# Order of weight conversions and splits in a retention, MLP and top-1 expert kernel

## The chip, the cores and the metric

The kernel runs on one core of a Trainium2 chip. TensorE (PE) multiplies matrices, VectorE (DVE), ScalarE (ACT) and GpSimd (POOL) work on elements, and SyncE (SP) issues most transfers. Each engine runs its own instructions in program order and waits for others by semaphores. The metric is the device time of one execution in microseconds. Before the change three runs took 579.2, 579.36 and 579.41 us.

## What is computed

Three stages in float32, each feeding the next; the weights `w_in` and `w_out` of the MLP come as float64.

```python
# retention attention, 2 batches x 8 heads, 768 positions, head size 64
intra = ((q @ k.T) * Dmask) @ v              # within a block of 64 positions
inter = (q * lam_pow) @ kv_state             # state carried over blocks
# MLP on x [1536, 512], hidden size 2048
h = maximum(x @ w_in, 0.0);  x = (h * h) @ w_out
# top-1 mixture of 8 experts, hidden size 1024
logits = x @ w_gate;  e_idx = argmax(logits, axis=1)
gate_w = softmax(logits)[arange(N), e_idx]
eom = 1 / (1 + exp(-(x @ w_output_gate)))
for e in range(8):
    mask = e_idx == e
    h = maximum(x[mask] @ w1[e], 0.0)
    out[mask] = gate_w[mask, None] * eom[mask, e, None] * (h @ w2[e])
```

## The kernel before

**Splitting.** To keep float32 accuracy, every operand of a big matmul is split in a high and a low part (`xTh`/`xTl`, `wih`/`wil`, `woh`/`wol`, `gh`/`gl`, `w1h`/`w1l`, `w2h`/`w2l`, `hh`/`hl`), and a product is three matmuls: high by high, low by high, high by low. A split is one cast on ScalarE (the high part) and one subtraction on VectorE or GpSimd (the low part), each 128 x 512.

**Attention** takes 12 units of 128 tokens and leaves its result, transposed and split, in `xTh` and `xTl` (512 rows in four pieces `kk` by 1536 token columns).

**MLP.** The tokens go in three chunks of 512 columns; the hidden size goes in 16 blocks `f` of 128. A step is s = 16 * chunk + f, 48 in all. `mm1(s)` is 12 matmuls (L339), `act1(s)` makes g = relu squared and splits it (L346 to L357), and `mm2(s - 2)` is 12 matmuls into four accumulators (L449), two steps behind. `split_in(s + 2)` splits a block of `w_in` (L326, L327) after `act1(s)`, `split_out(s)` a block of `w_out` within it.

**Conversion.** In the last units of attention and the first 12 steps of chunk 0 the float64 weights arrive in staging tiles `st` (SP, L107 and L110; four buffers) and are converted on the chip, two blocks a step: a scaled copy on ScalarE (L124), a shift (L125) and two combining operations on VectorE (L128 and L130, the second reads what the first wrote). The last two are kept in a list and run inside `act1` of the next step. From chunk 1 on no conversion is left, and `wol` is made by GpSimd.

**Routing.** Each chunk's result goes to memory as rows `x1d`, and the expert, position and slot of each token are worked out (`ohb`, `pos`, `pay`, `poh`, `sacc`, `sidx`, `gidx`). Tokens of an expert are fetched by indirect transfers of GpSimd (`xg`, L830), transposed by TensorE (`pt`, L850) and split into `xh`, `xl` (L855, L856) by `xpose`. For expert 0 the last tokens are picked by matmuls instead (`xt`, L717).

**Experts.** Each expert has eight blocks of 128 hidden units. `emm1(e, f)` (L884) makes `ph` in one of two PSUM buffers, then `hh` (ACT, L899) and `hl` (DVE, L900); `emm2(e, f - 2)` (L907) accumulates the output two blocks behind. The columns of `emm1` are 256 for expert 0, and 384, 256 or 192 by the token count for the others. `put` scales a result (L911) and scatters it to `out` (L912). `split1` and `split2` split the blocks of w1 and w2, each into one of 4 and 10 slots. Expert 0 also carries the rest of the routing of the last chunk in a table `late`, one list of jobs a block.

**Order.** All of it is written out by hand: an engine does its instructions in the order of the program. So an `hl` that waits for nothing still stands behind everything that VectorE was given before it.

Of the kernel before, what the change touches and what calls it, by code (L numbers as in the profile page):

```python
# [23 lines left out]
def attn_moe_kernel(ctx, tc, q, k, v, lam, w_in, w_out, w_gate, w_ogate, w1, w2, out):  # L24
# [367 lines left out]
    for u in range(NU):  # L394
# [361 lines left out]
    w1r, w2r = {}, {}
    NS = NCK * NF
    LAG = 2
    for s in range(NS + LAG):
# [19 lines left out]
        if s >= LAG:  # L779
# [82 lines left out]
    NS2 = E * NF2

    def split1(s, eng=nc.vector):
        if s < NS2:
            esplit(w1_of(*divmod(s, NF2)), *w1s[s % R1], eng)

    def split2(s, eng=nc.vector):
        if s < NS2:
# [4 lines left out]
    def emm1(e, f):
# [5 lines left out]
        def go(N):  # L880
            n = 0
            for kk in range(KC):
                for w_, x_ in ((w1h, xh), (w1h, xl), (w1l, xh)):
                    nc.tensor.matmul(out=ps[:, 0:N], lhsT=w_[:, kk, :], rhs=x_[:, kk, 0:N], start=n == 0,  # L884
                                     stop=n == 3 * KC - 1)
                    n += 1
# [41 lines left out]
    route_poh(ch, 0)  # L928
    route_poh(ch, 1)
    late = {0: [lambda: route_sum(ch), route_csb, lambda: route_poh(ch, 2)],  # L930
            1: [lambda: slot_mm(ch, [0, 1], 0, 2), lambda: slot_fin(ch, [0, 1], 0, 2), lambda: gathers(1, range(NSL))],
            2: [lambda: slot_mm(ch, [2], 0, 2), route_count, lambda: slot_fin(ch, [2], 0, 2), lambda: gathers(1, [NSL])],
            3: [lambda: route_gate(ch)],
            4: [lambda: route_gate1(ch)],
            5: [lambda: route_gate2(ch)],
            6: [lambda: slot_mm(ch, [0, 1], 2), lambda: slot_mm(ch, [2], 2), lambda: slot_fin(ch, [0, 1], 2),
                lambda: slot_fin(ch, [2], 2), lambda: route_gates(slice(0, NG))],
            7: [lambda: route_table(ch)]}
# [3 lines left out]
    def loads(s):  # L942

        while loaded[0] < NP and (loaded[0] // 2 < 4 or s + 3 >= (loaded[0] // 2 - 4) * 4 + 3):
            load_w1(loaded[0])
            loaded[0] += 1
        while loaded[1] < NP and (loaded[1] // 2 < 4 or s + 2 >= (loaded[1] // 2 - 4) * 4 + 3):
            load_w2(loaded[1])
            loaded[1] += 1
# [99 lines left out]
```

## Time and profile before

| what | value |
|---|---|
| median of three runs | 579.36 us |
| profiled execution | 580.5 us |
| its span, first to last instruction | 578.7 us |
| mean granted TensorE clock | 0.983 |
| TensorE busy | 552.3 us, 95% |
| VectorE busy | 374.0 us, 65% |
| ScalarE busy | 306.7 us, 53% |
| GpSimd busy | 153.9 us, 27% |

Busy time is the time in which an engine executes instructions; the waits of TensorE name the instruction that released it. A bracket at the end of a timeline row gives the idle time ahead of the instruction and its releaser. The granted clock is a share of full speed: 1 is 2.4 GHz, a half is 1.2 GHz.

### The profile page before, as it was taken

To read this page: it belongs to the slowest core of one execution; us is meant where nothing else is said; L and a number is where in the kernel's file an instruction comes from. 1 tells how busy PE (TensorE), PEld (TensorE's weight loads), DVE (VectorE), ACT (ScalarE), POOL (GpSimd) and SP (SyncE) were. 2 spreads that over 40 slices of the span, in tenths; PEclk is the share of its full clock that TensorE was granted. 3 is DMA by queue.
4 is the path that set the end of the run, shared out by engine and by line. 5 is a ranking of instruction groups with operands and counts; after the bars stand their busy time and mean duration, and the time that the engine had idled before them with its cause. 6 is when DMAs were issued, how large, how long until landed. Compare 5 with 4: busy or idle time off the path is not lost. (4 is left out here: it accounts for less than half of the span.)

```text
span 578.7 us, 9460 instructions
## 1 busy us (share of the span) xinstructions
PE 552.3 (95%) x3412; PEld 466.0 (81%) x3412; DVE 374.0 (65%) x744; ACT 306.7 (53%) x584; POOL 153.9 (27%) x153
## 2 busy tenths in 40 slices
PE   7999899999999999999999999899999999899994
PEld 6898777888777877887877887789898889888883
DVE  7579988998444665454565447965547649887430
ACT  4666476775544344434344335535456758886530
POOL 5788100000012132332113341223313132341101
PEclk8999998999999999999999999989999999999998
DMA  9999456568100001000000003975829477860000
GB/s 186 240 237 256 115 148 182 182 205 305 68 0 2 19 19 37 0 1 0 20 18 20 19 0 112 370 280 139 272 101 292 163 223 228 277 224 20 9 22 23
DMA packets 75043, 72.86 MB, mean 126 GB/s; under 512 B 30181, under 2 KB 61029, under 8 KB 74976
## 3 DMA queue, kind: packets, MB, share of 16 engines
q1 hardware_dynamic: 70624, 62.96, 36.9%
q0 software_dynamic: 4064, 8.91, 4.6%
q8 instruction: 42, 0.69, 0.5%
q14 instruction: 25, 0.20, 0.1%
q10 hardware_dynamic: 288, 0.10, 0.1%
HBM read 65.84 MB, written 9.29 MB: 130 GB/s over the span
## 5 line engine op out<-in xcount | busy, mean ns | idle before, releaser
L327 POOL TENSOR_TENSOR wol<-woF,woh 128x512 fp32r<-128x512 f32 x32 | 41.6, 1301 | 231.9 <-ACT woh L326 231.9
L357 DVE TENSOR_TENSOR gl<-g,gh 128x512 fp32r<-128x512 f32 x48 | 53.6, 1116 | 70.4 <-ACT gh L356 70.4
L884 PE MATMUL ph<-xh,w1h 128*128 128x192 f32 (+2 forms) x256 | 76.4, 299 | 6.0 <-PEq L1013 2.5
L339 PE MATMUL ps<-xTh,wil 128*128 128x512 f32 x192 | 76.7, 399 | 1.9 <-DVE wil L327 1.9
L339 PE MATMUL ps<-xTh,wih 128*128 128x512 f32 x192 | 77.9, 406 | 0.0
L339 PE MATMUL ps<-xTl,wih 128*128 128x512 f32 x192 | 76.5, 398 | 0.0
L449 PE MATMUL acc<-gh,woh 128*128 128x512 f32 x192 | 76.1, 396 | 0.3 <-DVE x1T L461 0.2
L449 PE MATMUL acc<-gl,woh 128*128 128x512 f32 x192 | 75.8, 395 | 0.0
L449 PE MATMUL acc<-gh,wol 128*128 128x512 f32 x192 | 75.8, 395 | 0.0
L884 PE MATMUL ph<-xl,w1h 128*128 128x192 f32 (+2 forms) x256 | 74.9, 293 | 0.1
L884 PE MATMUL ph<-xh,w1l 128*128 128x192 f32 (+2 forms) x256 | 74.9, 293 | 0.0
L900 DVE SCALAR_TENSOR_TENSOR hl<-ph,hh 128x384 fp32r<-128x384 f32 (+1 forms) x64 | 34.5, 539 | 61.8 <-ACT hh L899 60.8
L326 ACT CAST woh<-woF 128x512 fp32r<-128x512 f32 x48 | 29.7, 619 | 64.6 <-PE acc L449 62.3
L884 PEld LDWEIGHTS ph<-xh,w1h 128*128 128x128 f32 x256 | 48.9, 191 | 9.9 <-issue 6.1
L899 ACT ACTIVATE hh<-ph 128x384 fp32r<-128x384 f32 (+1 forms) x64 | 30.7, 479 | 45.0 <-PE ph L884 43.0
L346 ACT ACTIVATE r<-ps 128x512 f32<-128x512 f32 x48 | 28.5, 593 | 44.1 <-PE ps L339 44.1
L907 PE MATMUL ea<-w2h,hh 128*128 128x512 f32 x128 | 51.4, 402 | 0.0
L907 PE MATMUL ea<-w2l,hh 128*128 128x512 f32 x128 | 50.4, 394 | 0.0
L907 PE MATMUL ea<-w2h,hl 128*128 128x512 f32 x128 | 50.3, 393 | 0.0
L884 PEld LDWEIGHTS ph<-xl,w1h 128*128 128x128 f32 x256 | 48.8, 191 | 1.5 <-DVE xl L856 0.3
L860 DVE TENSOR_TENSOR w2l<-w2r,w2h 128x512 fp32r<-128x512 f32 x71 | 49.1, 691 | 0.2
L912 POOL DMA_INDIRECT out_dram<-y,sidx x23 | 24.3, 1058 | 93.3 <-ACT y L911 51.3
(177 smaller groups left out, 1135.3 us busy)
## 6 DMA issues: line engine op xcount, KB each, us to landing
w1r<-in_moe_w_dram SPq DMA_DIRECT2D x32, 512.0 KB, 5.8
w2r<-in_moe_w_dram SPq DMA_DIRECT2D x32, 512.0 KB, 6.7
st<-in_moe_w_in_dram SPq DMA_DIRECT2D x16, 512.0 KB, 3.8
st<-in_moe_w_out_dram SPq DMA_DIRECT2D x16, 512.0 KB, 4.8
q<-in_q_dram SPq DMA_DIRECT2D x24, 128.0 KB, 4.1
k<-in_k_dram SPq DMA_DIRECT2D x12, 256.0 KB, 4.6
v<-in_v_dram SPq DMA_DIRECT2D x12, 256.0 KB, 5.4
x1d<-xr SPq DMA_DIRECT2D x12, 256.0 KB, 2.0
```

What stands on the lines that cost most here:

```text
L326: nc.scalar.copy(out=hi, in_=src)
L327: eng.tensor_tensor(out=lo, in0=src, in1=hi.bitcast(F32), op=ALU.subtract)
L339: nc.tensor.matmul(out=ps, lhsT=w_[:, kk, :], rhs=x_[:, kk, tk], start=n == 0, stop=n == 3 * KC - 1)
L346: nc.scalar.activation(out=r, in_=ps, func=AF.Relu)
L357: nc.vector.tensor_tensor(out=gl, in0=g, in1=gh.bitcast(F32), op=ALU.subtract)
L449: nc.tensor.matmul(out=acc[ch][cb], lhsT=w_[:, cs], rhs=x_, start=f == 0 and i == 0, stop=f == NF - 1 and i == 2)
L860: eng.tensor_tensor(out=lo, in0=src, in1=hi.bitcast(F32), op=ALU.subtract)
L884: nc.tensor.matmul(out=ps[:, 0:N], lhsT=w_[:, kk, :], rhs=x_[:, kk, 0:N], start=n == 0, stop=n == 3 * KC - 1)
L899: nc.scalar.activation(out=hh[:, f, ts_], in_=ps[:, ts_], func=AF.Relu)
L900: nc.vector.scalar_tensor_tensor(out=hl[:, f, ts_], in0=ps[:, ts_], scalar=0.0, in1=hh[:, f, ts_].bitcast(F32), op0=ALU.max, op1=ALU.subtract)
L907: nc.tensor.matmul(out=ea[j], lhsT=h_[:, f, js], rhs=w_, start=f == 0 and i == 0, stop=f == NF2 - 1 and i == 2)
L912: nc.gpsimd.indirect_dma_start(out=out[:, :], out_offset=bass.IndirectOffsetOnAxis(ap=sidx[:, j, e:e + 1], axis=0), in_=ys[j], in_offset=N ...
```

## The change

1. `conv_w` returns the two combining operations apart, and `flush` runs the first ones of both conversions and then the second ones.
2. In steps 2 to 15, `split_in(s + 2)` runs inside `act1(s)`, after `split_out(s)` and ahead of `flush`.
3. `xTh` and `xTl` outlive the MLP. The slots of `split1` and eight of the ten of `split2` are parts of them: token columns whose chunk is done. The first four blocks of w1 and of w2 of expert 0 are split in steps 33 to 40, in the third chunk of the MLP (`ch` = 2); the subtraction is then `xTl<-w1r,xTh`.
4. In the expert loop `splits_to` splits w1 four blocks ahead and up to two blocks of w2 after each `emm1`, as far as ten blocks of w2 from the expert's start; loads follow what is split.
5. Expert 0: the matmuls of `emm1(0, 0)` that read `xl` come after those of the same pair of `kk` that read `xh`; all `poh` and the counts stand ahead of the block loop; one `slot_mm`, `slot_fin` and gather job for all three groups, in block 1; the gate in blocks 2 and 3; `xpose(1, 0)` and `xpose(1, 1)` in blocks 6 and 7 and `xpose(1, 2)` after the last `emm2`.
6. The scatters to `out` and `tab` go through disjoint views of them, so that they do not wait for each other.

```diff
+    outs = dram_disjoint_views(out, NG)
+    tabs = dram_disjoint_views(tab, 4)
+    xp = ctx.enter_context(tc.tile_pool(name="xp", bufs=1))
+    xTh = xp.tile([P, KC, NT], F32R, name="xTh")
+    xTl = xp.tile([P, KC, NT], F32R, name="xTl")
...
-        def rest():
+        def shifted():
             nc.vector.scalar_tensor_tensor(out=sh(lo), in0=dst.bitcast(U32), scalar=3, in1=sh(lo),
                                            op0=ALU.logical_shift_left, op1=ALU.bitwise_or)
+
+        def signed():
             nc.vector.scalar_tensor_tensor(out=dst.bitcast(U32), in0=sh(hi), scalar=0x80000000, in1=sh(lo),
                                            op0=ALU.bitwise_and, op1=ALU.bitwise_or)
-        return rest
+        return shifted, signed
...
+    def flush():
+        for step in range(2):
+            for r_ in rest_:
+                r_[step]()
+        rest_.clear()
...
-            nc.gpsimd.indirect_dma_start(out=tab[:, :], out_offset=bass.IndirectOffsetOnAxis(ap=sl[:, t, :], axis=0),
+            nc.gpsimd.indirect_dma_start(out=tabs[t][:, :], out_offset=bass.IndirectOffsetOnAxis(ap=sl[:, t, :], axis=0),
...
+    R1, R2 = 4, 10
+    room = [[x_[:, kk, c * NTC:(c + 1) * NTC] for x_ in (xTh, xTl)] for c in range(NCK) for kk in range(KC)]
+    w1s = [[t_.rearrange("p (k f) -> p k f", k=KC) for t_ in room[i]] for i in range(R1)]
+    w2s = room[R1:]
...
-                act1(s, lambda: (split_out(s), flush()))
+                early = 2 <= s < NF
+                act1(s, lambda: (split_out(s), split_in(s + 2) if early else None, flush()))
         if s == 0:
             split_in(3)
-        elif 2 <= s < NS - 2:
+        elif NF <= s < NS - 2:
             split_in(s + 2)
...
+        if s - 2 * NF in range(1, 9):
+            i, j = divmod(s - 2 * NF - 1, 2)
+            (split1, split2)[j](i)
...
+            mms = [(kk, w_, x_) for kk in range(KC) for w_, x_ in ((w1h, xh), (w1h, xl), (w1l, xh))]
+            if s == 0:
+                mms.sort(key=lambda m: (m[0] // 2, m[2] is xl))
...
-    split1(0)
-    split1(1)
-    split2(0)
     xpose(0, 0)
-    split1(2)
     xpose(0, 1)
...
-    route_poh(ch, 0)
-    route_poh(ch, 1)
-    late = {0: [lambda: route_sum(ch), route_csb, lambda: route_poh(ch, 2)],
-            1: [lambda: slot_mm(ch, [0, 1], 0, 2), lambda: slot_fin(ch, [0, 1], 0, 2), lambda: gathers(1, range(NSL))],
-            2: [lambda: slot_mm(ch, [2], 0, 2), route_count, lambda: slot_fin(ch, [2], 0, 2), lambda: gathers(1, [NSL])],
...
+    for j in range(NG):
+        route_poh(ch, j)
+    route_sum(ch)
+    route_csb()
+    late = {1: [lambda: slot_mm(ch, list(range(NG)), 0, 2), route_count, lambda: slot_fin(ch, list(range(NG)), 0, 2),
+                lambda: gathers(1, range(NG))],
+            2: [lambda: route_gate(ch), lambda: route_gate1(ch)],
+            3: [lambda: route_gate2(ch)],
...
+    done = [4, 4]
+
+    def splits_to(n1, n2):
+        while done[0] < min(n1, NS2):
+            split1(done[0])
+            done[0] += 1
+        while done[1] < min(n2, NS2):
+            split2(done[1])
+            done[1] += 1
...
-            split2(s + 1)
-            split1(s + 3)
-            if f == NF2 - 1:
-                split2(s + 2)
-            loads(s if f < NF2 - 1 else s + 1)
+            splits_to(s + 5, min(s + 5, done[1] + 2, e * NF2 + R2))
+            loads()
...
-            if e + 1 < E and f >= 5:
-                xpose(e + 1, f - 5)
...
+            if f >= 5 + (e == 0):
+                rows_of(e + 1, f - 5 - (e == 0))
```

VectorE in one step of MLP chunk 0 with conversions, before the change: `wol` and `wil` are the splits, `st` and `wiF`/`woF` the combining operations (L128, L130) and the shifts (L125).

```order
L327 TENSOR_TENSOR wol<-woF,woh 128x512
L128 SCALAR_TENSOR_TENSOR st<-wiF,st 128x512
L130 SCALAR_TENSOR_TENSOR wiF<-st 128x4x128
L128 SCALAR_TENSOR_TENSOR st<-woF,st 128x512
L130 SCALAR_TENSOR_TENSOR woF<-st 128x512
L357 TENSOR_TENSOR gl<-g,gh 128x512
L327 TENSOR_TENSOR wil<-wiF,wih 128x512
L125 TENSOR_SCALAR st<-st 128x512 x2
```

The same step of the changed kernel.

```order
L335 TENSOR_TENSOR wol<-woF,woh 128x512
L335 TENSOR_TENSOR wil<-wiF,wih 128x512
L134 SCALAR_TENSOR_TENSOR st<-wiF,st 128x512
L134 SCALAR_TENSOR_TENSOR st<-woF,st 128x512
L138 SCALAR_TENSOR_TENSOR wiF<-st 128x4x128
L138 SCALAR_TENSOR_TENSOR woF<-st 128x512
L365 TENSOR_TENSOR gl<-g,gh 128x512
L131 TENSOR_SCALAR st<-st 128x512 x2
```

`wil` has moved from behind `gl` to the place after `wol`, ahead of the four combining operations, and the pairs of these are interleaved.

VectorE at the start of expert 0, before: weight splits (L860) stand between the two `xl`, eight of the twelve `poh` ahead of the first `hl`.

```order
L860 TENSOR_TENSOR w2l<-w2r,w2h 128x512
L856 TENSOR_TENSOR xl<-xt_3576,xh 128x2x256
L860 TENSOR_TENSOR w1l<-w1r,w1h 128x512
L856 TENSOR_TENSOR xl<-xt_3595,xh 128x2x256
L521 TENSOR_SCALAR pay<-ohb,pp_96 128x4x8
L522 TENSOR_TENSOR pay<-ohb,tix 128x4x8
L587 TENSOR_SCALAR poh<-slots,pos 128x128 x8
L900 SCALAR_TENSOR_TENSOR hl<-ph,hh 128x256
L860 TENSOR_TENSOR w2l<-w2r,w2h 128x512
L860 TENSOR_TENSOR w1l<-w1r,w1h 128x512
```

The same place of the changed kernel; the splits of weights are the rows of L777.

```order
L885 TENSOR_TENSOR xl<-xt_3595,xh 128x2x256
L885 TENSOR_TENSOR xl<-xt_3614,xh 128x2x256
L535 TENSOR_SCALAR pay<-ohb,pp_96 128x4x8
L536 TENSOR_TENSOR pay<-ohb,tix 128x4x8
L601 TENSOR_SCALAR poh<-slots,pos 128x128 x12
L541 TENSOR_REDUCE csum<-ohb 128x8
L660 CAST csb<-csum 128x8
L915 SCALAR_TENSOR_TENSOR hl<-ph,hh 128x256
L777 TENSOR_TENSOR xTl<-w1r,xTh 128x512
L777 TENSOR_TENSOR xTl<-w2r,xTh 128x512
```

No weight split is left ahead of the first `hl`, and all twelve `poh` and the counts stand there.

VectorE in the first blocks of a later expert, before and then in the changed kernel.

```order
L900 SCALAR_TENSOR_TENSOR hl<-ph,hh 128x384
L860 TENSOR_TENSOR w2l<-w2r,w2h 128x512
L891 UNCONDITIONAL_BRANCH
L860 TENSOR_TENSOR w1l<-w1r,w1h 128x512
L900 SCALAR_TENSOR_TENSOR hl<-ph,hh 128x384
```

```order
L915 SCALAR_TENSOR_TENSOR hl<-ph,hh 128x384
L777 TENSOR_TENSOR xTl<-w1r,xTh 128x512
L906 UNCONDITIONAL_BRANCH
L777 TENSOR_TENSOR xTl<-w2r,xTh 128x512 x2
L915 SCALAR_TENSOR_TENSOR hl<-ph,hh 128x384
```

Two splits stand between two `hl` before, three in blocks 0 and 1 now.

## Rows read from the trace of the kernel before

**Rows 1.** Waits of TensorE: line, releaser, us in total, times, longest.

```profile
PE pt L850 <- DMA xg<-x1d,gidx: 2.1, 2, 1.1
...
PE pt L609 <- DVE sacc L620: 1.1, 1, 1.1
```

**Rows 2.** Timeline of TensorE, step 4 of chunk 0: start, us, operation, idle before.

```profile
87.72 0.50 PE L339 MATMUL ps<-xTh,wil 128*128 128x512 f32 x1 [1.94 <-DVE wil L327]
...
88.65 0.63 PE L339 MATMUL ps<-xTh,wil 128*128 128x512 f32 x1
...
91.64 0.46 PE L449 MATMUL acc<-gh,woh 128*128 128x512 f32 x1
```

**Rows 3.** Windows: from:to, length, busy of each engine, PEclk, DMA share, GB/s.

```profile
300.00:315.00 15.00, 15.00 (x74) 11.84 (x74) 9.55 (x24) 7.14 (x13) 3.84 (x3) 1.00 0.10 36
360.00:370.00 10.00, 7.84 (x66) 7.18 (x67) 9.77 (x34) 4.73 (x11) 0.97 (x1) 1.00 0.95 322
379.00:382.00 3.00, 3.00 (x23) 2.38 (x22) 2.76 (x9) 1.41 (x3) 0.00 (x0) 0.51 1.07 387
```

**Rows 4.** Timeline of VectorE, steps 2 and 4 of chunk 0.

```profile
83.10 0.69 DVE L327 TENSOR_TENSOR wol<-woF,woh 128x512 fp32r<-128x512 f32 x1 [0.59 <-ACT woh L326]
83.71 0.69 DVE L128 SCALAR_TENSOR_TENSOR st<-wiF,st 128x512 uint32<-128x512 uint32 x1
84.44 0.69 DVE L130 SCALAR_TENSOR_TENSOR wiF<-st 128x512 uint32<-128x512 uint32 x1
...
86.98 0.69 DVE L327 TENSOR_TENSOR wil<-wiF,wih 128x512 fp32r<-128x512 f32 x1
...
95.95 0.69 DVE L327 TENSOR_TENSOR wol<-woF,woh 128x512 fp32r<-128x512 f32 x1 [1.95 <-ACT woh L326]
```

**Rows 5.** Timeline of TensorE, the start of mm1(6) and of mm2(4).

```profile
100.11 0.40 PE L339 MATMUL ps<-xTh,wih 128*128 128x512 f32 x1
...
103.00 0.39 PE L449 MATMUL acc<-gh,woh 128*128 128x512 f32 x1
```

**Rows 6.** Timeline of ScalarE, chunk 0.

```profile
93.57 0.69 ACT L124 ACTIVATE woF<-st 128x512 f32<-128x512 f32 x1 [3.40 <-DMA st<-in_moe_w_out_dram]
```

**Rows 7.** Timeline of ScalarE ahead of expert 0.

```profile
358.74 0.59 ACT L855 CAST xh<-xt 128x512 fp32r<-128x512 f32 x1 [1.42 <-PE xt L717]
```

**Rows 8.** Timeline of TensorE, expert 0 and the start of expert 1.

```profile
360.93 0.38 PE L884 MATMUL ph<-xh,w1h 128*128 128x256 f32 x1 [1.27 <-DVE xl L856]
...
371.73 0.40 PE L907 MATMUL ea<-w2h,hh 128*128 128x512 f32 x1
...
373.86 0.40 PE L907 MATMUL ea<-w2h,hh 128*128 128x512 f32 x1
...
391.29 0.33 PE L884 MATMUL ph<-xh,w1h 128*128 128x384 f32 x1
```

**Rows 9.** Timeline of VectorE, expert 0.

```profile
362.22 1.39 DVE L587 TENSOR_SCALAR poh<-slots,pos 128x128 bf16<-128x128 int16 x8
...
377.42 0.16 DVE L559 CAST gb<-gt 128x4 bf16<-128x4 f32 x1
...
379.16 0.68 DVE L856 TENSOR_TENSOR xl<-pt,xh 128x512 fp32r<-128x512 f32 x1
```

**Rows 10.** DMA issues: queue, times, median us from issue to landing.

```profile
xg<-x1d,gidx POOLq DMA_INDIRECT x21, 6.7
```

**Rows 11.** Timeline of VectorE at the start of expert 5.

```profile
496.06 0.56 DVE L900 SCALAR_TENSOR_TENSOR hl<-ph,hh 128x384 fp32r<-128x384 f32 x1 [1.84 <-ACT hh L899]
496.57 0.69 DVE L860 TENSOR_TENSOR w2l<-w2r,w2h 128x512 fp32r<-128x512 f32 x1
```

**Rows 12.** Timeline of TensorE at the start of expert 5, first matmuls of two blocks.

```profile
493.92 0.36 PE L884 MATMUL ph<-xh,w1h 128*128 128x192 f32 x1 [0.72 <-PEq L1009]
...
495.34 0.28 PE L884 MATMUL ph<-xh,w1h 128*128 128x192 f32 x1
```

**Rows 13.** Timeline of GpSimd, the last scatter.

```profile
572.08 0.98 POOL L912 DMA_INDIRECT out_dram<-y,sidx  x1 [3.62 <-ACT y L911]
```

More of the change, by code (lines that the diff above doesn't have):

```diff
@@ L5 @@
 from concourse import mybir
+from concourse.bass_types import dram_disjoint_views
 from concourse._compat import with_exitstack
@@ L816, in attn_moe_kernel @@
     ea = [pe_a.tile([P, DM], F32, tag=f"ea{j}", name="ea") for j in range(NG)]
-    R1, R2 = 4, 10
-    w1s = [[ep.tile([P, KC, P], F32R, tag=f"w1{t_}{i}", name=f"w1{t_}") for t_ in "hl"] for i in range(R1)]
-    w2s = [[ep.tile([P, DM], F32R, tag=f"w2{t_}{i}", name=f"w2{t_}") for t_ in "hl"] for i in range(R2)]
+    w2s += [[ep.tile([P, DM], F32R, tag=f"w2{t_}{i}", name=f"w2{t_}") for t_ in "hl"] for i in range(len(w2s), R2)]
     xs_ = [[ep.tile([P, KC, NX], F32R, tag=f"x{t_}{i}", name=f"x{t_}") for t_ in "hl"] for i in range(2)]
@@ L880, in go @@
         def go(N):
[L881 to L886, printed above, removed]
+            mms = [(kk, w_, x_) for kk in range(KC) for w_, x_ in ((w1h, xh), (w1h, xl), (w1l, xh))]
+            if s == 0:
+                mms.sort(key=lambda m: (m[0] // 2, m[2] is xl))
+            for n, (kk, w_, x_) in enumerate(mms):
+                nc.tensor.matmul(out=ps[:, 0:N], lhsT=w_[:, kk, :], rhs=x_[:, kk, 0:N], start=n == 0,
+                                 stop=n == 3 * KC - 1)
         if e == 0:
@@ L927, in attn_moe_kernel, with loads, rows_of @@
     route_pay(ch)
-    route_poh(ch, 0)
-    route_poh(ch, 1)
-    late = {0: [lambda: route_sum(ch), route_csb, lambda: route_poh(ch, 2)],
-            1: [lambda: slot_mm(ch, [0, 1], 0, 2), lambda: slot_fin(ch, [0, 1], 0, 2), lambda: gathers(1, range(NSL))],
-            2: [lambda: slot_mm(ch, [2], 0, 2), route_count, lambda: slot_fin(ch, [2], 0, 2), lambda: gathers(1, [NSL])],
[L933 to L938, printed above, removed]
+    for j in range(NG):
[6 more added lines that the diff above has]
+            3: [lambda: route_gate2(ch)],
+            6: [lambda: slot_mm(ch, list(range(NG)), 2), lambda: slot_fin(ch, list(range(NG)), 2),
+                lambda: route_gates(slice(0, NG)), lambda: route_table(ch)]}
     loaded = [4, 4]
     NP = NS2 // 2
[L942 to L949, printed above, removed]
+    done = [4, 4]
[6 more added lines that the diff above has]
+            done[1] += 1
+    def loads():
+        for w, load in enumerate((load_w1, load_w2)):
+            while loaded[w] < NP and (loaded[w] // 2 < 4 or done[w] > (loaded[w] // 2 - 4) * 4 + 3):
+                load(loaded[w])
+                loaded[w] += 1
+    def rows_of(e, g):
+        if e < E:
+            xpose(e, g)
+            if e + 1 < E and g > 0:
+                gathers(e + 1, range(NSL) if g == 1 else [NSL])
     def beyond():
@@ L996, in attn_moe_kernel @@
             if e == 0:
-                for job in late[f]:
+                for job in late.get(f, ()):
                     job()
-            if e + 1 < E and f >= 5:
-                xpose(e + 1, f - 5)
-                if e + 2 < E:
-                    gathers(e + 2, {6: range(NSL), 7: [NSL]}.get(f, ()))
+            if f >= 5 + (e == 0):
+                rows_of(e + 1, f - 5 - (e == 0))
             if e == 0 and f == NF2 - 1:
@@ L1007, in attn_moe_kernel @@
             emm2(e, f, 0)
+        if e == 0:
+            rows_of(1, 2)
         put(e, 0)
```

28 lines of the change are left out of this document (10 added, 18 removed).

## The prediction

> **What bounds the kernel now.** I read the waits of TensorE first, then the timelines of TensorE and VectorE around the longest of them, then the table of windows for the clock. TensorE is the bound almost everywhere; the reader should see that behind attention only a few of its stalls are a microsecond or more, and that the change touches four places: `wil` in chunk 0 [rows 2], `xl` at expert 0's start [rows 8], `sacc` and the gathered rows `xg` in expert 0 [rows 1]. All but the last name VectorE as releaser.
>
> The first is at step 4 of MLP chunk 0. Two matmuls of mm1(4) run, then TensorE waits 1.94 us for `wil` [rows 2]. After that the matmuls come 0.43 us apart (88.65 to 91.64 are seven steps, 2.99 us [rows 2]), where the twelve of mm1(6) take 2.89 us, 0.24 each [rows 5]. That is the lower of the two clock levels, 1.2 instead of 2.4 GHz. Eight matmuls at 0.43 - 0.24 cost 1.5 us, so this place costs 1.94 + 1.5 = 3.4 us.
>
> The second is expert 0: 1.27 us for `xl` [rows 8], 1.12 us for `sacc`, two waits of together 2.1 us for `xg` [rows 1]. After the gather stalls the granted clock is 0.51 over three microseconds [rows 3], a further loss of (1 - 0.51) x 3 = 1.5 us. Together 6.0 us.
>
> **Parts 1 and 2, chunk 0.** VectorE does in a step s `wol`(s), four conversion operations, `gl`(s), `wil`(s + 2) and two shifts. `wil`(4) stood at 86.98, 3.88 us after `wol` [rows 4]; `wol`'s slot is 0.61 us long (83.10 to 83.71), and now `wil` follows it: it ends at 83.71 + 0.69 = 84.4. TensorE began to wait for it at 87.72 - 1.94 = 85.8 [rows 2]. The stall goes, and with it what came before the fall of the clock. Gain 3.4. On ScalarE `gh` now stands behind `wih`, one cast later; mm2 reads it a whole mm1 later, so that costs nothing.
>
> Part of the gain comes back. TensorE reaches mm1(6) 3.4 us earlier, at 100.11 - 3.4 = 96.7 [rows 5], and needs `wil`(6) two matmuls later, at 97.2. But the chain ahead of it does not depend on TensorE: ScalarE's conversion at 93.57 stood idle for 3.40 us until a weight load had landed [rows 6], and `wol` at 95.95 follows from that, idle for 1.95 us [rows 4]. The staging buffer of a load comes free with the last conversion step on it, and these now stand behind one more `wil` (0.6), so the loads go out some 0.3 to 0.6 us later. `wol` then stands at about 96.4, and `wil`(6) ends at 96.4 + 0.61 + 0.69 = 97.7: 0.5 us late. `gl`(4) is behind `wil` and four conversion steps now, so it ends some 3 us after `wil`(6), and makes mm2(4) about 0.3 us late. I take 0.8 us returned; the ends are 0 and 3.4 (a stall as long as the one removed, and the clock falling again). Net -2.6.
>
> The order of the four conversion steps by itself: the second of a dependent pair starts 0.73 us after the first (83.71 to 84.44), where neighbours that do not depend start 0.61 apart (83.10 to 83.71) [rows 4]. Interleaving two pairs saves about 2 x 0.11 us a step on VectorE, and it is in the 0.3 above. The Trainium skill, "VectorE: DVE Perf Modes", section "The DRAIN you can't avoid", says that a dependence between chained operations adds nothing, since the pipeline empties after each anyway. By that rule interleaving saves nothing, `gl`(4) is 0.5 late instead of 0.3, and the sum is 0.2 worse; these rows speak against it.
>
> **Part 3, four blocks split in the third chunk.** Eight casts and eight subtractions move from expert 0 into steps 33 to 40. One window there has VectorE busy 9.55 us and ScalarE 7.14 us of 15 [rows 3]; eight times 0.6 over some 45 us fit. They wait for no matmul that is still to come, since the slots lie in token columns of chunks 0 and 1. Cost 0. If that cover were gone, one slot of 0.6 us a step would come on the path, 4.8 us at most.
>
> **Part 5, expert 0.** ScalarE made `xh` at 358.74, released by TensorE [rows 7]; with no weight split ahead of it, `xl`(0) can follow at 359.33 and end at 360.0, so emm1(0,0) starts at 360.05 instead of 360.93 [rows 8]. The stall shrinks from 1.27 to 0.4. New waits come, all on VectorE, since the whole slot search now stands ahead of the first `hl`. A block takes 2.13 us (371.73 to 373.86 [rows 8]), of which emm2's three matmuls are 0.7 and emm1 1.43; in blocks 0 and 1 there is no emm2.
> - `xl`(1) ends at about 361.0; two `pay`, twelve `poh` (eight took 1.30 from 362.22, 0.16 each [rows 9]) and two small ones bring it to 363.65, and `hl`(0) ends at 364.1. TensorE has two emm1 and twelve short matmuls until 363.55. emm1(0,2) waits for `hl`(0), since it takes its PSUM buffer, and with it all later TensorE work: stall 0.55.
> - `hl`(2) is behind two splits, the counts and the slot chain and ends at about 368.55; TensorE is there at 368.4: 0.2.
> - `hl`(3) is behind two more splits and the first half of the gate, with an exponential on ScalarE (about 1.6), and ends at 371.65; TensorE is there at 370.75: 0.9.
> - `hl`(4) is behind two splits and the gate's second half, 379.16 - 377.42 = 1.74 [rows 9], and ends at 374.95; TensorE is there at 373.85: 1.1.
>
> New stalls are 0.4 + 0.55 + 0.2 + 0.9 + 1.1 = 3.15. The slot index is ready at about 368.2, so three gathers go out from 368.4 to 371.1 and land 6.7 us later [rows 10], from 375.1 to 377.8. The first transpose comes at about 377.8 now, and the last one only after emm2: both gather stalls go. Each new stall has a full block or more behind it. After the 1.27 and 1.12 us stalls, each by itself, the clock stayed at 1.00 (360 to 370 [rows 3]), so I assume no fall. Net 3.15 - 6.0 = -2.85. Ends: -5 (most of the VectorE waits vanish) and +0.2 (the clock falls twice).
>
> **Part 4, splits in experts 1 to 7.** In blocks 0 and 1 three splits stand behind an `hl` instead of two. Where an expert has 192 columns, `hl`'s slot is 0.51 us [rows 11] and a split's 0.6, so VectorE needs 0.51 + 3 x 0.6 = 2.3 us, where an emm1 takes 1.42 [rows 12]. VectorE starts with slack (its first `hl` came after 1.84 us of idling [rows 11]) and catches up from block 2 on, where emm2 adds 0.7; going through the blocks, `hl`(2) is about 0.2 us late for emm1(4). Experts 3 to 6 are such: 0.8 us; the others have longer blocks. I take +0.8, ends 0 and +7.2 (the whole lag of 2 x 0.9 us in four experts).
>
> **Part 6, disjoint views.** Scatters no longer wait for each other's landing on GpSimd. The last one, at 572.08, was released by ScalarE's `y` [rows 13], so the end gains nothing; those of the table stand beside TensorE work. Cost 0.
>
> **Sum.** -2.6 - 2.85 + 0.8 = -4.65. The profiled execution took 580.5 us (its span of 578.7 and 1.8 around it), so 575.85 by its own time; it was 1.1 above the median of the runs, 579.36, from which the forecast is 574.7.
>
> **The rivals.**
> - B, chunk 0 gives most of it back. For it: the load chain idles ScalarE for 3.40 us already [rows 6]. If mm1(6) waits as mm1(4) did, the clock falls and 3.4 comes back instead of 0.8: 577.3. Against it: `wil`(6) no longer stands behind `gl` and four conversion steps either.
> - C, expert 0 keeps a low clock. For it: 0.9 and 1.1 us stand close together, as the two gather stalls did, or the gathers land 1 us later among the weight loads and stall too. Price 1.5 to 3: about 577.
> - D, slower. The front-loaded splits become a bound of the 192-column experts: 7.2 instead of 0.8, so 574.7 + 6.4 = 581.1. It decides as soon as these four lose over 5.5 us together, 1.4 each. Against it: an `hl` is needed only two blocks later.
> - E, better: 2 us of the 3.15 in expert 0 don't show, as VectorE gains there what it no longer splits: 572.7.
> - F, the change does not do what part 3 says: the splits hit TensorE in steps 33 to 40 after all, by up to 4.8: 579.5. VectorE's idle share there speaks against it.
>
> **How the numbers follow.** Forecast 0.50, B 0.14, C 0.12, D 0.08, E 0.13, F 0.03. A measurement of this kernel can tell about 0.2%, 1.2 us. Faster by more than that are the forecast, E and nearly all of B and C: 0.86. Within it: F and the upper tails of B and C, 0.06. Slower: D, 0.08. The range runs from beyond E (571.0) to just above B and C (577.8).
>
> **What would show it.** Right: no idle ahead of `wil` in mm1(4) and a granted clock near 1.0 there and in expert 0; short idles at mm1(6); TensorE waiting for `hl`, not for `xg`, in expert 0; expert 1 starting some 5.5 us earlier than 391.29 [rows 8]. Wrong: a clock of about 0.5 further on in chunk 0 or in expert 0, over 0.5 us of waits in each 192-column expert, or waits of TensorE in steps 33 to 40.

## The result, and the profile after

Four runs of the changed kernel took 572.56, 573.02, 573.35 and 574.58 us, median 573.18; the kernel before beside them 579.38. The ratio is 0.9896, with a 95% interval of 0.9876 to 0.9916: 6.2 us faster, where 4.65 were forecast. 573.18 lies within the range, 1.5 us below the forecast of 574.7. Three of the 69 executions of the kernel before that were timed beside the experiments (585.6, 587.3 and 615.5 us) were slow ones and stand in no range below.

The first matmuls of four places, read from the timelines of both profiled executions, split the difference of the spans (578.7 and 571.6 us):

| stage, by first matmul | before | after | difference | forecast |
|---|---|---|---|---|
| start to the last `po` of attention | 68.96 | 67.80 | -1.16 | 0 |
| to the first matmul of expert 0 (MLP) | 291.97 | 287.33 | -4.64 | -2.6, and -0.9 for `xl` |
| expert 0 | 30.36 | 27.54 | -2.82 | -1.95 |
| experts 1 to 7 and the end | 187.41 | 188.93 | +1.52 | +0.8 |

The first row is not the change's: in the profiled execution of before the granted clock was 0.85 and 0.90 in the first two stretches of 14 us, after it was 1.00. That execution was 1.1 us above its median, about as much as this row. The others add up to -5.94.

The waits of TensorE after (line, releaser, us in all, times, longest). `wil`, `sacc` and `xg` [rows 1, 2] are gone from the list; `hl` is new.

```profile
PE ph L900 <- DVE hl L915: 1.8, 3, 0.9
...
PE ph L900 <- DVE xl L885: 0.5, 1, 0.5
```

Chunk 0 of the MLP, timeline of VectorE after, one step (start, us, operation, idle before and releaser). These rows are to be read beside [rows 4].

```profile
85.32 0.68 DVE L365 TENSOR_TENSOR gl<-g,gh 128x512 fp32r<-128x512 f32 x1
85.92 0.76 DVE L131 TENSOR_SCALAR st<-st 128x512 uint32<-128x512 uint32 x2
87.27 0.69 DVE L335 TENSOR_TENSOR wol<-woF,woh 128x512 fp32r<-128x512 f32 x1 [0.59 <-ACT woh L334]
87.88 0.69 DVE L335 TENSOR_TENSOR wil<-wiF,wih 128x512 fp32r<-128x512 f32 x1
88.48 0.69 DVE L134 SCALAR_TENSOR_TENSOR st<-wiF,st 128x512 uint32<-128x512 uint32 x1
89.08 0.69 DVE L134 SCALAR_TENSOR_TENSOR st<-woF,st 128x512 uint32<-128x512 uint32 x1
89.69 0.68 DVE L138 SCALAR_TENSOR_TENSOR wiF<-st 128x512 uint32<-128x512 uint32 x1
90.29 0.68 DVE L138 SCALAR_TENSOR_TENSOR woF<-st 128x512 uint32<-128x512 uint32 x1
90.89 0.68 DVE L365 TENSOR_TENSOR gl<-g,gh 128x512 fp32r<-128x512 f32 x1
```

All of them start 0.60 or 0.61 us apart: no 0.73 between dependent ones is left. From `gl` to `gl` are 5.57 us. ScalarE does its part of the step between, and there its next `g` waits for `gl`:

```profile
86.09 0.64 ACT L357 ACTIVATE g<-r 128x512 f32<-128x512 f32 x1 [0.68 <-DVE gl L365]
86.64 0.60 ACT L334 CAST woh<-woF 128x512 fp32r<-128x512 f32 x1
```

The windows after (from:to, length, busy of PE, PEld, DVE, ACT, POOL, PEclk, DMA share, GB/s) show no stall in this part of chunk 0 and the clock at 1.00 there and in expert 0, where it had been 0.51 [rows 3].

```profile
75.00:90.00 15.00, 15.00 (x66) 12.09 (x65) 12.63 (x24) 10.85 (x21) 0.00 (x0) 1.00 0.41 141
360.00:370.00 10.00, 8.34 (x56) 6.93 (x55) 9.12 (x39) 5.66 (x13) 3.35 (x4) 1.00 1.07 397
370.00:375.00 5.00, 5.00 (x47) 4.51 (x47) 4.64 (x12) 2.05 (x5) 4.08 (x4) 1.00 1.05 403
```

Expert 0, timeline of TensorE after, to be read beside [rows 8]: its four waits, the transposes of gathered rows, which wait for nothing now, and expert 1.

```profile
355.13 0.39 PE L900 MATMUL ph<-xh,xTh 128*128 128x256 f32 x1 [0.45 <-DVE xl L885]
...
358.94 0.39 PE L900 MATMUL ph<-xh,xTh 128*128 128x256 f32 x1 [0.16 <-DVE hl L915]
...
366.50 0.39 PE L900 MATMUL ph<-xh,xTh 128*128 128x256 f32 x1 [0.78 <-DVE hl L915]
...
369.77 0.39 PE L900 MATMUL ph<-xh,xTh 128*128 128x256 f32 x1 [0.88 <-DVE hl L915]
...
372.32 0.64 PE L879 MATMUL pt<-ident,xg 128*128 128x128 f32 x4
...
382.67 0.33 PE L900 MATMUL ph<-xh,xTh 128*128 128x384 f32 x1
```

Experts 1 to 7 cost 1.5 us more without any new wait in the list, since the new waits are short. VectorE in expert 3 (192 columns), the splits of block 0, `hl`(1) and the first split of block 1:

```profile
445.29 0.69 DVE L777 TENSOR_TENSOR xTl<-w1r,xTh 128x512 fp32r<-128x512 f32 x1
445.90 1.29 DVE L777 TENSOR_TENSOR xTl<-w2r,xTh 128x512 fp32r<-128x512 f32 x2
447.10 0.55 DVE L915 SCALAR_TENSOR_TENSOR hl<-ph,hh 128x384 fp32r<-128x384 f32 x1
447.57 0.68 DVE L777 TENSOR_TENSOR xTl<-w1r,xTh 128x512 fp32r<-128x512 f32 x1
```

and TensorE beside it, the last matmul of emm2(3, 0) and the first of emm1(3, 3):

```profile
447.29 0.40 PE L922 MATMUL ea<-xTh,hl 128*128 128x512 f32 x1
447.71 0.36 PE L900 MATMUL ph<-xh,xTh 128*128 128x192 f32 x1
```

`hl`(1) ends at 447.65, and the block that takes over its PSUM buffer starts at 447.71, 0.42 us after the matmul before it instead of 0.23. A gap of 0.2 us has no bracket in a timeline; it is seen in the starts. The next block starts 0.14 us late in the same way. The three other experts of 192 columns show the same two gaps, 0.17 to 0.19 and 0.13 us; over the four they make 1.3 us.

The 1.52 us of the table are a net sum. The kernel before had a wait in expert 5 that the changed kernel has not:

```profile
497.67 0.33 PE L884 MATMUL ph<-xh,w1h 128*128 128x192 f32 x1 [0.83 <-ACT hh L899]
```

So besides the gaps at `hl` some 1.1 us more were lost elsewhere, in gaps that were not followed one by one.

### The profile page after: what moved, and what is told of

It reads as the page before. It is cut to its first block, busy times and chain, and to the rows that moved or that the text cites. A ratio compares the mean times of both kernels' runs of the same rounds, so it can differ in the third digit from the quotient of the medians.

```text
span 571.6 us, 9445 instructions
## 1 busy us (share of the span) xinstructions
PE 549.3 (96%) x3412; PEld 461.5 (81%) x3412; DVE 364.4 (64%) x731; ACT 304.0 (53%) x577; POOL 151.6 (27%) x153
## 5 line engine op out<-in xcount | busy, mean ns | idle before, releaser
L900 PE MATMUL ph<-xh,xTh 128*128 128x192 f32 (+2 forms) x256 | 77.6, 303 | 6.6 <-issue 2.3
L900 PE MATMUL ph<-xh,xTl 128*128 128x192 f32 (+2 forms) x256 | 74.7, 292 | 0.0
L900 PE MATMUL ph<-xl,xTh 128*128 128x192 f32 (+2 forms) x256 | 74.4, 292 | 0.0
L900 PEld LDWEIGHTS ph<-xh,xTh 128*128 128x128 f32 x256 | 48.7, 190 | 15.2 <-DVE hl L915 7.3
L900 PEld LDWEIGHTS ph<-xl,xTh 128*128 128x128 f32 x256 | 48.7, 191 | 0.7
L900 PEld LDWEIGHTS ph<-xh,xTl 128*128 128x128 f32 x256 | 48.8, 191 | 0.0
L859 POOL DMA_INDIRECT xg<-x1d,gidx x21 | 23.5, 1117 | 89.1 <-PE pt L879 66.1
L777 DVE TENSOR_TENSOR xTl<-w1r,xTh 128x512 fp32r<-128x512 f32 x64 | 44.1, 689 | 0.1
L463 PEld LDWEIGHTS acc<-gh,woh 128*128 128x128 f32 x192 | 36.0, 188 | 9.8 <-DVE x1T L475 1.2
```

The source lines that it names most:

```text
L463: nc.tensor.matmul(out=acc[ch][cb], lhsT=w_[:, cs], rhs=x_, start=f == 0 and i == 0, stop=f == NF - 1 and i == 2)
L859: nc.gpsimd.indirect_dma_start(out=out_, out_offset=None, in_=x1d[:, :], in_offset=bass.IndirectOffsetOnAxis(ap=ix, axis=0), bounds_check= ...
```

## Experiments

Each is an edit of the changed kernel except one (e4), and was timed beside the kernel before, in three sets on three chips: e1 to e4; the changed kernel again with e5, e6 and e7; e9 to e12. The changed kernel itself was timed in the second set only. For the other sets it stands here by its two medians, 573.18 and 574.05 us, which were not taken beside them. The kernel before took 576.2 to 581.7 us (median 579.9) beside the first set, with a mean granted clock from 0.997 down to 0.985, so ratios to it are wide, and stages are compared in the profiles, by the same first matmuls as in the table above.

**The changed kernel again.** No edit.

> The changed kernel itself, nothing edited, timed again beside the others of this set, since on the chip of the first set the kernel before spread from 576.2 to 581.7 us with a mean granted clock from 0.997 down to 0.985. If the spread of before is falls of the clock behind its long stalls, and the changed kernel has lost these stalls, its times stay within about 2.5 us (572.5 to 575) with a mean clock of 0.99 or more; if the spread belongs to the chip, it spreads over 5 us as well.

574.05 us median (573.15 to 576.40), ratio 0.9904 (0.9867 to 0.9941), clock 0.993 to 0.996; before took 576.3 to 584.6 beside it, at 0.985 to 0.997. The spread was wider than expected, by the one run at 576.40, but the clock stayed high. The clock is not all of the spread of before: two of its executions took 578.84 and 579.55 us at 0.997, and one 584.61 at 0.992. In the profile the MLP took 287.32 us and expert 0 27.49, as in the first profile (287.33 and 27.54). Experts 1 to 7 took 189.55 (188.93), so in that stage 0.6 us can lie between two executions of one kernel.

**e1: `wil` behind the conversions again.**

```diff
-                early = 2 <= s < NF
+                early = False
...
-        elif NF <= s < NS - 2:
+        elif 2 <= s < NS - 2:
```

> The changed kernel, but wil(s + 2) is again made behind the conversions and gl, as before the change; the interleaving of the conversions stays. Theory 1 (the place of wil is the whole gain of chunk 0): TensorE waits about 1.5 to 1.9 us for wil in mm1(4), the clock falls to 0.5 behind it, and the time goes back by 3.2 to 3.8 us, from 573.2 to 576.4 to 577.0. Theory 2 (the shorter conversions alone would do, since they bring wil forward by only 2 x 0.11 us a step): the wait shrinks below 1.0 us, no fall of the clock, 573.8 to 574.3.

575.18 us (574.38 to 576.33), ratio 0.9938 (0.9917 to 0.9959): 1.1 to 2.0 us slower than the changed kernel. The MLP stage takes 289.00 us, 1.67 more. TensorE waits again, but without a fall of the clock in this execution:

```profile
85.82 0.50 PE L347 MATMUL ps<-xTh,wil 128*128 128x512 f32 x1 [1.45 <-DVE wil L335]
```

```profile
85.00:95.00 10.00, 9.18 (x39) 7.42 (x40) 9.74 (x19) 8.23 (x15) 0.00 (x0) 1.00 0.60 211
```

Neither theory got it all: the place of `wil` makes the wait, as theory 1 says; interleaving shortened it from 1.94 to 1.45 us; and the fall did not come in the profiled execution.

**e2: the operations of a conversion behind each other again.**

```diff
-        for step in range(2):
-            for r_ in rest_:
-                r_[step]()
+        for r_ in rest_:
+            for step in range(2):
+                r_[step]()
```

> The changed kernel, but the two operations of one conversion stand behind each other again, as before the change; wil stays ahead of them. Theory 1 (VectorE is not the bound of chunk 0 once wil is early): the dependent pairs are 0.72 us apart instead of 0.60, VectorE needs 0.22 us more a step and nothing else changes: 573.0 to 573.4. Theory 2 (VectorE is the bound of the load chain, so that its steps add up over 12 steps and reach mm1 or mm2): waits of TensorE in chunk 0 of 0.2 to 1.0 us, 573.4 to 574.2.

576.57 us (575.32 to 578.14), ratio 0.9963 (0.9944 to 0.9982): 2.5 to 3.4 us slower than the changed kernel, more than theory 2 expected. The MLP takes 289.31 us, 1.98 more, and no wait of it is in the list: in each of the eight steps from 104 to 145 us two matmuls that read or follow `gl` are 0.10 to 0.14 us late (one is 0.22 late), which adds up to 1.9 us. The medians lost 0.5 to 1.4 us more than this stage, and no stage shows where. Here 115.44 to 115.81 is 0.37 us and the next 0.33, where 0.23 is usual:

```profile
115.44 0.39 PE L463 MATMUL acc<-gh,woh 128*128 128x512 f32 x1
115.81 0.50 PE L463 MATMUL acc<-gl,woh 128*128 128x512 f32 x1
116.14 0.39 PE L463 MATMUL acc<-gh,wol 128*128 128x512 f32 x1
```

From `gl` to `gl` on VectorE are 5.83 us now:

```profile
109.24 0.68 DVE L365 TENSOR_TENSOR gl<-g,gh 128x512 fp32r<-128x512 f32 x1
...
115.07 0.69 DVE L365 TENSOR_TENSOR gl<-g,gh 128x512 fp32r<-128x512 f32 x1
```

VectorE idles 0.59 us in it, waiting for `woh`, so it is not simply full. The next experiment asks what the loop is made of.

**e5: as e2, with `g` made in place in a tile of two buffers.**

```diff
-        r = gp[0].tile([P, NTC], F32, tag="r", name="r", bufs=1)
+        r = gp[0].tile([P, NTC], F32, tag="r", name="r", bufs=2)
...
-        g = gp[0].tile([P, NTC], F32, tag="g", name="g", bufs=1)
+        g = r
```

> The changed kernel with the two operations of a conversion behind each other (as in e2, which lost 2 us in chunk 0 with gl some 0.12 + 0.10 us late in each step), and the square of relu made in place in a tile with two buffers, so that g of a step no longer waits until gl of the step before has read its buffer. Theory 1 (a loop of 5.8 us over gl, g, woh, wol, wil, four conversion operations and gl again, against 5.58 us of TensorE a step, is what e2 lost to): the loop is cut, the gaps at gl go, 573.0 to 573.8. Theory 2 (VectorE simply has too much to do in a step): the gaps stay, 575.3 to 576.5.

574.11 us (573.41 to 576.08), ratio 0.9906 (0.9876 to 0.9936), as the changed kernel beside it; the MLP takes 287.30 us, and the late matmuls are gone although the dependent pairs still stand 0.72 apart. Theory 1 holds: with one buffer `g` of a step waits until `gl` of the step before has read it, then follow `woh`, `wol`, `wil`, four operations and `gl`. Moving `wil` ahead of `gl` put its 0.60 us into this loop, which was 5.23 us in the kernel before (`gl` at 81.15 and 86.38) and is 5.83 in e2. In the changed kernel it is 5.57, just below the 5.60 us of TensorE's step: it fits only because interleaving took 0.22 out.

**e4: parts 1 and 2 alone, on the kernel before.** The edits are those of `conv_w`, `flush` and `act1` in the diff of the change.

> The kernel before with parts 1 and 2 alone (wil early, conversions interleaved). Theory 1 (chunk 0 and expert 0 add up): chunk 0 gives 3.4 to 3.9 us by itself, 575.5 to 576.0. Theory 2 (as predicted, part of it comes back at mm1(6)): 576.4 to 577.0, with waits of TensorE in chunk 0.

576.11 us (574.16 to 579.45), ratio 0.9953 (0.9927 to 0.998). The MLP takes 288.15 us, 3.82 less than before: the gain of theory 1, nothing returned at mm1(6); the median is 0.1 above its range. The order in expert 0 is that of before the change, and TensorE waits for gathered rows:

```profile
371.40 0.33 PE L854 MATMUL pt<-ident,xg 128*128 128x128 f32 x1 [1.39 <-DMA xg<-x1d,gidx]
...
372.43 0.55 PE L854 MATMUL pt<-ident,xg 128*128 128x128 f32 x3 [0.70 <-DMA xg<-x1d,gidx]
```

but the clock after that was at 1.00 in this execution, where it had been at 0.51 [rows 3]. Expert 0 took 28.93 us in it, 1.43 less than the 30.36 of the table, with its order unchanged. The window behind the two waits:

```profile
373.00:376.00 3.00, 3.00 (x34) 2.69 (x34) 2.83 (x15) 2.07 (x5) 0.00 (x0) 1.00 1.04 393
```

**e7: no splits in steps 33 to 40.** Three blocks of w1 and one of w2 ahead of and between the transposes again, the rest in blocks 0 and 1.

```diff
-        if s - 2 * NF in range(1, 9):
-            i, j = divmod(s - 2 * NF - 1, 2)
-            (split1, split2)[j](i)
...
+    split1(0)
+    split1(1)
+    split2(0)
     xpose(0, 0)
+    split1(2)
     xpose(0, 1)
...
-    done = [4, 4]
+    done = [3, 1]
```

> The changed kernel without the splits in steps 33 to 40: three blocks of w1 and one of w2 are split ahead of and between the transposes of expert 0, as before the change, the other four in its first two blocks; all else as changed. Theory 1 (moving the splits to the third chunk is what makes room on VectorE in expert 0): the wait for xl is 1.3 us again and hl in blocks 0 to 3 comes 1 to 2.4 us later, the time rises by 2.5 to 4 us to 575.7 to 577.2. Theory 2 (the gain in expert 0 comes from the new order of the slot search and gather alone): plus 0.8 us for xl and at most 0.5 more, 574 to 574.5.

577.29 us (576.54 to 577.89), ratio 0.995 (0.9923 to 0.9976): 3.2 us slower than the changed kernel beside it. Theory 1 holds. Expert 0 takes 30.17 us (27.54), the MLP with `xl` 0.80 more; the waits for `hl` grow as the queue on VectorE does:

```profile
356.77 0.39 PE L897 MATMUL ph<-xh,xTh 128*128 128x256 f32 x1 [1.27 <-DVE xl L882]
...
367.01 0.39 PE L897 MATMUL ph<-xh,xTh 128*128 128x256 f32 x1 [1.05 <-DVE hl L912]
...
370.79 0.39 PE L897 MATMUL ph<-xh,xTh 128*128 128x256 f32 x1 [1.38 <-DVE hl L912]
...
374.05 0.39 PE L897 MATMUL ph<-xh,xTh 128*128 128x256 f32 x1 [0.86 <-DVE hl L912]
```

**e11: the early splits, with expert 0's jobs in their old blocks.** The table `late`, the `poh` and the blocks of `xpose` are those of the kernel before.

> The changed kernel with expert 0's jobs in their old blocks (slot search and gathers in two parts, the gate in blocks 3 to 5, transposes of gathered rows from block 5 on), the splits in steps 33 to 40 kept. Theory 1 (the early splits and the new order need each other): TensorE waits for gathered rows again, 1 to 2.5 us in all, in some executions with a fall of the clock behind it, 574.5 to 576. Theory 2 (the early splits alone give the gain in expert 0): 573 to 574, no wait for xg above 0.5 us.

576.81 us (575.69 to 578.11), ratio 0.993 (0.9899 to 0.996): 2.8 to 3.6 slower than the changed kernel, above the range of theory 1, which holds. Expert 0 takes 29.76 us. The wait for `sacc` and those for gathered rows are back, and one for `pay` is new, which neither theory had:

```profile
362.80 0.25 PE L623 MATMUL pt<-pay,poh 128*128 128x16 bf16 x4 [1.11 <-DVE sacc L634]
...
371.04 0.33 PE L879 MATMUL pt<-ident,xg 128*128 128x128 f32 x1 [1.49 <-DMA xg<-x1d,gidx]
372.06 0.55 PE L879 MATMUL pt<-ident,xg 128*128 128x128 f32 x3 [0.69 <-DMA xg<-x1d,gidx]
375.69 0.45 PE L623 MATMUL pt<-pay,poh 128*128 128x24 bf16 x12 [0.96 <-DVE pay L574]
```

Parts 3 and 5 need each other. Neither profile, e7 or e11, has a fall of the clock in expert 0, so they are to be compared with the 28.93 us of e4, which has none either, and not with 30.36: either part alone makes expert 0 longer by 0.8 to 1.2 us, and only both together bring it to 27.54. (The early splits also take 0.82 us off the wait for `xl` ahead of expert 0, so in all e11 neither gains nor loses there.)

**e10: no disjoint views.**

```diff
-    outs = dram_disjoint_views(out, NG)
-    tabs = dram_disjoint_views(tab, 4)
+    outs = [out] * NG
+    tabs = [tab] * 4
```

> The changed kernel with the scatters to the output and the table through the plain tensors, so that they wait for each other's landing again. Theory 1 (as predicted, these waits stand beside TensorE's work): within 0.5 us of the changed kernel, 573 to 574.5. Theory 2 (GpSimd's gathers for expert 2 stand behind the table scatters and come too late): TensorE waits for xg in expert 1, 1 to 3 us more.

581.18 us (576.28 to 582.02), ratio 0.9999 (0.9972 to 1.0025): the whole gain is gone, more than theory 2 gave it. (Nine of the twelve runs took 579.7 to 582.0 us, the other three 576.3 to 577.8; the profile is of one of the nine.) Experts 1 to 7 take 196.36 us, 7.43 more. On GpSimd each table scatter waits for the one before it, and all gathers for expert 2 stand behind them:

```profile
370.44 1.55 POOL L594 DMA_INDIRECT tab<-tg,sl  x1 [2.82 <-DVE tg L588]
380.26 0.98 POOL L594 DMA_INDIRECT tab<-tg,sl  x1 [8.28 <-DMA tab<-tg,sl]
386.99 1.31 POOL L594 DMA_INDIRECT tab<-tg,sl  x1 [5.75 <-DMA tab<-tg,sl]
392.89 0.97 POOL L594 DMA_INDIRECT tab<-tg,sl  x1 [4.59 <-DMA tab<-tg,sl]
394.16 1.19 POOL L859 DMA_INDIRECT xg<-x1d,gidx  x1 [0.30 <-issue]
```

so that TensorE waits for their rows in expert 1, and the clock falls:

```profile
401.05 0.33 PE L879 MATMUL pt<-ident,xg 128*128 128x128 f32 x1 [2.09 <-DMA xg<-x1d,gidx]
404.11 0.90 PE L879 MATMUL pt<-ident,xg 128*128 128x128 f32 x3 [2.74 <-DMA xg<-x1d,gidx]
```

```profile
402.00:405.00 3.00, 0.89 (x4) 0.89 (x5) 0.00 (x0) 0.00 (x0) 0.00 (x0) 0.50 1.03 387
```

In the kernel before, two gathers for expert 2 went out ahead of the table scatters, at 382.13 and 383.44, and the scatters' waits cost nothing. Part 5 put the table's job ahead of all three. The views of `out` were not taken out by themselves; the scatters to it wait too (up to 7.42 us on GpSimd), but TensorE has no further wait for `xg`.

**e3: one w2 split a block in experts 1 to 7.**

```diff
-            splits_to(s + 5, min(s + 5, done[1] + 2, e * NF2 + R2))
+            splits_to(s + 5, min(s + 5, done[1] + (2 if e == 0 else 1), e * NF2 + R2))
```

> The changed kernel, but experts 1 to 7 split one block of w2 after each emm1 instead of two in blocks 0 and 1 and none in blocks 6 and 7. Theory 1 (the hl behind three splits is late for emm1(3) and emm1(4)): the gaps of 0.1 to 0.2 us there go, experts 2 to 6 lose about 0.35 us less each, and the time falls by 1.0 to 1.6 us to 571.6 to 572.2. Theory 2 (the 1.5 us come from elsewhere, from the issue of instructions at the branches): 573.0 to 573.4. Theory 3 (a split in blocks 6 and 7 makes the next expert's xl late): experts start 0.3 us later each, 573.5 to 575.

571.04 us (570.24 to 572.32; every run below every run of the changed kernel), ratio 0.9871 (0.9839 to 0.9903). Experts 1 to 7 take 186.70 us, 2.23 less than in the changed kernel and 0.7 less than before the change, where the wait of 0.83 us for `hh` stood. The gaps at `hl` are gone from all four experts of 192 columns. Theory 1, with more than was expected.

**e6: relief for VectorE in expert 0.** The w2 splits begin in block 4, the last two come behind the expert; the gate's jobs stand in blocks 2, 3 and 4.

```diff
+            splits_to(s + 5, (4, 4, 4, 4, 5, 6, 7, 8)[f] if e == 0 else min(s + 5, done[1] + 2, e * NF2 + R2))
...
+            2: [lambda: route_gate(ch)],
+            3: [lambda: route_gate1(ch)],
+            4: [lambda: route_gate2(ch)],
```

> The changed kernel; in expert 0 the w2 splits begin in block 4 instead of block 0 (it has four ready), the last two come behind its last block, and the gate's three jobs stand in blocks 2, 3 and 4 instead of 2, 2 and 3. Theory 1 (hl queues on VectorE behind splits and gate jobs, stalls of 0.78 and 0.88 us): these two stalls shrink to under 0.4 us together, the time falls by 1.2 to 1.6 us to 571.6 to 572.0. Theory 2 (the stalls move to later blocks, where three splits now stand behind hl and xl): within 0.4 us of the changed kernel.

573.23 us (572.31 to 574.34), ratio 0.9887 (0.9847 to 0.9927): 0.8 us below the changed kernel beside it, not told apart by the intervals and between the two theories. In the profile expert 0 takes 26.06 us, 1.48 less: both waits of 0.78 and 0.88 are gone, and a new one has come, for the split of block 7, now too late:

```profile
374.57 0.50 PE L922 MATMUL ea<-xTl,hh 128*128 128x512 f32 x1 [0.58 <-DVE xTl L777]
```

**e9 and e12: both.** e9 joins e3 and e6, with the list (4, 4, 4, 5, 6, 7, 8, 8); e12 adds the two buffers of e5.

> The changed kernel with one w2 split a block in experts 1 to 7 (as in e3) and, in expert 0, w2 splits from block 3 on (4, 4, 4, 5, 6, 7, 8, 8 done after its blocks, the last two behind the expert's blocks) and the gate's jobs in blocks 2, 3 and 4 (as in e6, which ran into a late split of block 7, 0.58 us). If the two queues on VectorE are separate, their gains add: 1.5 to 2.1 from the experts and 1.3 to 1.6 from expert 0, 570 to 571 where the changed kernel takes 573.2 to 574.0. If one takes the place of the other, 571 to 572.5.

> e9 with the square of relu in place in a tile of two buffers, as in e5. If the loop over gl and g in chunk 0 (5.57 us beside 5.58 of TensorE) costs nothing in the changed kernel, it is within 0.5 us of e9; if it costs something in some executions, 0.5 to 1 us faster and a narrower spread.

e9: 571.34 us (570.17 to 574.36), ratio 0.9842 (0.981 to 0.9873). e12: 570.87 (569.92 to 574.24), ratio 0.9838 (0.9806 to 0.9871). Both are faster than before, and their medians lie below those of the changed kernel, but against e3 alone (571.04, in another set) no further gain can be told. The profiles tell only part of why, since each is of the slowest run of its six, 3.0 and 3.4 us above the median. In them expert 0 takes 25.35 and 25.23 us, 2.2 and 2.3 less than in the changed kernel, yet a wait in expert 1 takes that back (e9; 2.03 us in e12, at the same matmul):

```profile
393.43 0.79 PE L922 MATMUL ea<-w2h,hh 128*128 128x512 f32 x1 [2.39 <-ACT xTh L776]
```

The cast that is named had ended at 392.59 and is not an operand, so what it waited for is open, and so is whether the faster runs have it. The same matmul was 0.31 to 0.40 us late in the second profile of the changed kernel, in e5 and in e6, with no releaser. Behind the wait of e9 the granted clock was 0.50 (393.4 to 396.6), behind that of e12 it stayed at 1.00 (394.9 to 398.0). e12 against e9 shows no effect of the two buffers that can be told.

## Why the prediction was right, and where it was not

**Chunk 0 (forecast -2.6, measured -3.8).** The gain was there, and a little larger than the 3.4 us it was priced at. From start to start, the wait held TensorE up by 2.2 us (87.72 comes 2.33 us after the matmul before it, where 0.23 is usual, and the next is 0.10 late) and the low clock cost 1.5; with 0.08 us at 100.58 this is all of the 3.8. The 0.8 us returned at mm1(6) was the mis-sized term: nothing came back (after and e4). I had left the chain of weight loads where it stood in one step of before, with a conversion 3.40 us late [rows 6], which ran 7.05 us after its load went out at 86.52. In the changed kernel the conversions of `w_out` that wait for their load run at most 4.42 us after it went out, and ScalarE waits at most 0.56 us. Nor do both loads of a step go out later, as I had it. Of the two that went out at 79.97 and 81.30 before, counted from the last `po`, that of `w_in` goes out 0.48 us later, but that of `w_out`, the one waited for, 0.25 earlier: with the interleaving the two buffers come free 0.60 us apart and not 1.33. One late landing in a trace is not a chain.

**The interleaving (costed inside 0.3).** Wrong by an order: without it `wil`'s new place costs 2.0 us in the profile (e2). I counted VectorE's idle time and did not close the loop through ScalarE's `g`: 5.57 us against 5.60 of TensorE (24 matmuls at 0.233). The reading of [rows 4], 0.73 us against 0.61, was right: with interleaving all are 0.60 to 0.61 apart, and those 0.22 us a step were what made the change fit. The Trainium skill, "VectorE: DVE Perf Modes", section "The DRAIN you can't avoid", says that a semaphore between chained operations costs nothing extra. The rows speak against it, as the prediction said.

**Expert 0 (forecast -2.85 with `xl`, measured -3.64).** The mechanism was right in each step: no wait for `xg`, waits of 0.45, 0.16, 0.78 and 0.88 us for `xl` and `hl` where 0.4, 0.55, 0.2, 0.9 and 1.1 were worked out, and no fall of the clock. Two sizes were too high: the 0.55 and 0.2 us for `hl`(0) and `hl`(2) came out as 0.16 and nothing, and the stalls add up to 2.27 us instead of 3.15. e7 and e11 show that the early splits and the new order give this only together.

**Experts 1 to 7 (forecast +0.8, measured +1.5).** Right in mechanism, a late `hl` behind three splits, and too small: in all four experts of 192 columns emm1(3) and emm1(4) are late, 0.3 us together, not emm1(4) alone by 0.2. The rest of the loss was not foreseen. e3 takes all of it back.

**Disjoint views (costed at nothing).** Here the reason given was wrong: the table scatters stand beside TensorE's work only as long as the gathers of expert 2 do not stand behind them. Part 5 put them there, and without the views the change gives nothing (e10). The sum came out right because the views are part of the change; that is luck, not reckoning.

**The clock.** The falls behind the wait of 1.94 us and behind those of 1.06 and 1.04 us were treated as certain. They are not: behind 1.45 us (e1), 1.39 and 0.70 us (e4) and 2.03 us (e12) the granted clock stayed at 1.00. Of the 5.94 us between the two profiles about 3 are such falls, which the profile of before happened to have: 1.5 in chunk 0, and the 1.43 by which expert 0 took longer than in e4. What the removed waits are worth by themselves is an estimate from these profiles: 2.2 us in chunk 0 and 2.2 in expert 0 with `xl` (28.93 + 0.82 - 27.54), less the 1.5 lost in the later experts, 2.9 us. The fastest executions of the two kernels in the second set, 576.29 and 573.15 us, lie 3.1 apart, which fits. So about half of the 6.2 us would be the waits and half the falls behind them, which come in a part of the executions; no run separates the two.

Of the rivals, B, C and F did not come; D was the mechanism of part 4 at a fifth of its price. The result lies between the forecast and E, but E's mechanism, stalls of expert 0 that do not show, gave 0.9 us and not 2; the rest came from chunk 0.

## What to carry to other kernels

Before moving an operation ahead of another on a busy engine, close the loop that it enters, from a buffer's reader through the other engines back to that reader, and compare its length with the bound engine's period: idle time on the engine does not show the slack. A wait that costs nothing has an amount of cover, and it must be named with what stands behind it in the new order, not in the old. Gaps of 0.1 to 0.2 us have no bracket and no entry in a list of waits; they are seen in the starts of a step, and the sixteen of e2 are 1.9 us. A profile is one execution: before a fall of the clock in it is counted as a gain, other executions should show it too.

## What the runs showed of the hardware

- VectorE: an operation on 128 x 512 starts 0.72 to 0.73 us after one it depends on and 0.60 to 0.61 after one it does not, all 32-bit forms of [rows 4].
- TensorE's clock: after waits of 1.45 us (e1), of 1.39 and 0.70 us (e4) and of 2.03 us (e12) the granted clock stayed at 1.00; after 1.94 us and after 1.06 and 1.04 us (before), after 2.09 and 2.74 us (e10) and after 2.39 us (e9) matmuls ran at the lower level, 1.2 GHz. The length of the wait alone does not tell the two apart. The kernel before had a mean clock from 0.985 to 0.997 in the executions of the first set, and took 581.7 to 576.2 us.
- Indirect scatters to one table that wait for each other's landing went out 9.8, 6.7 and 5.9 us apart while weights were loaded (e10); through disjoint views, 1.5 to 1.9 us apart (369.67, 371.52, 373.01 and 374.53, after).
